# Other places for the softmax pieces of head pairs 6 to 8 in the first feed-forward batch of a fused attention and feed-forward kernel

## The chip, the core and the metric

One NeuronCore of a Trainium2 chip runs the whole program. The metric is the device time of one execution in microseconds (us); a kernel is told by the median of its runs. In the profile PE is TensorE (matmuls; PEld its weight loads), DVE is VectorE, ACT is ScalarE, POOL is GpSimd and SP is SyncE, which here issues most of the DMAs. L127 is line 127 of the kernel.

## The reference, cut to what matters

The attention has 8 batches, 8 heads, 512 local and 32 global positions and a head dimension of 64. A local position attends to the local positions within 32 of it and to the 32 global ones, a global position to all 544. The result goes through a feed-forward network with a softplus between its two products, all in float32.

```python
s_ll = scale * np.matmul(q_l, k_l.transpose(0, 1, 3, 2))
s_ll = np.where(mask, s_ll, -1000000000.0)        # |pos - pos'| <= 32
s_l = np.concatenate([s_lg, s_ll], axis=-1)
out_l = np.matmul(sm(s_l), np.concatenate([v_g, v_l], axis=2))
...
x = np.ascontiguousarray(attn_out.transpose(0, 2, 1, 3)).reshape(B * S, H * D)
h = x @ w_in                                       # 4352 x 512 by 512 x 2048
g = np.maximum(h, 0.0) + np.log1p(np.exp(-np.abs(h)))
return g @ w_out                                   # 4352 x 2048 by 2048 x 512
```

## The kernel before, in words

**Pairs and batches.** The 64 (batch, head) attentions are done two at a time: 32 head pairs, four to a batch of the feed-forward network. Pairs 0 to 5 are computed first, in a loop of their own. Pairs 6 to 31 are each cut into five *pieces*, which are written between the parts of the feed-forward work. Feed-forward batch 0 uses pairs 0 to 3, batch 1 pairs 4 to 7, batch 2 pairs 8 to 11; so pairs 6 and 7 have to be finished while batch 0 runs, and pair 8 while batch 1 runs.

**The pieces of a pair m** (list built in `pieces`, lines 425 to 446):
- `scores(m, 0)` and `scores(m, 1)` (L296): TensorE computes half of the scores each into `s_ps`, two banks of PSUM. For pairs 6 and 7 the mask is added by a matmul and ScalarE copies the half to the tile `s` (L322); for pair 8 VectorE adds the mask as it copies (L327). VectorE then takes maxima of blocks (L333). With each half go the loads of pair m+1's queries and keys (L288).
- `maxima(m)` and `probs(m, 0)`, `probs(m, 1)` (L364, L371): GpSimd moves the block maxima together (L354), VectorE folds them (L357 to L367) and spreads them into two tiles `mb` (L375); GpSimd subtracts them from `s` in seven instructions (L379), ScalarE exponentiates each half (L381), VectorE sums blocks (L385).
- `totals(m)` (L388): the same fold for sums, the reciprocals (L354, L357 to L361, L390, L391, L394) and `rb` (L396).
- `values(m)` and `normalise(m)` (L398, L411): TensorE multiplies by the values into `v_ps`; VectorE reads `v_ps` in L416, L417 and L418 and finishes in L419 and L421.

From the moment the feed-forward output banks exist, `s_ps` (of pairs up to 8) and `v_ps` take turns in one and the same pair of PSUM banks (pool `ps_a`, one buffer). So scores that are written behind a `values` can start only when L418 has read the values out.

**Feed-forward.** For each of 16 feature blocks f of a batch, TensorE computes `h_f` in two halves of six matmuls (`hpart`, L532), into two PSUM buffers taken in turn. ScalarE computes Abs, Exp and Ln into a tile `e` (L550 to L552), VectorE finishes softplus in L553, which is also the last reader of `h_f`: the matmuls of `h_f+2` wait for it. ScalarE rounds `e` to `gh` (L556), GpSimd computes the rest `gl` (L558), and the output products `o` of that block (`opart`, L561), twelve matmuls, read `gh` and `gl`; below, o(f) is that group of twelve. In batch 0 the writing order is h_0, h_1, h_2, o(0), h_3, o(1) and so on: one h, one o.

**Weights.** During the attention of pairs 0 to 5 and through batch 0, the weights are cut into a high and a low part, one tile of 128x512 after the other: a load by SP (L475), a ScalarE copy (L489), three VectorE instructions (L496, L498, L501, each on a 128x512 tile, called `wbits` and `raw`), a ScalarE rounding (L506) and two GpSimd subtractions (L508). Sixteen tiles are written before batch 0; the others are written in between the parts of batch 0, by lines 641 to 652 and 713.

**What sets the order.** Each piece has a number, its place; `SLOTS` (line 38) gives the five numbers of pairs 6, 7 and 8 in the order first scores, second scores, maxima with probabilities, totals, values. In batch 0 a running value `at` goes from 76 to 103.5 as the feed-forward parts are written, in batch 1 from 103.5 to 151.5, and a piece is written once `at` has reached its number:

```python
        at = first + 48 * (b + gone[b] / total[b]) if b else START + (first + 48 - START) * gone[b] / total[b]
        while pcs and pcs[0][0] <= at:
            pcs.pop(0)[1]()
```

Places under 76 (72 and 75 of pair 6) are taken in the loop before. The matmuls keep the order in which they are written (L126), and so do the loads of queries, keys and weights among themselves. Everything else is arranged by the framework's scheduler, which decides the row of each engine's instructions from the program, from the buffers and from its own estimates of time. The resulting row of each engine is fixed at build time; an instruction that waits holds up what stands behind it in its engine's row.

Of the kernel before, what the change touches and what calls it, by code (L numbers as in the profile page):

```python
# [34 lines left out]
TOT = 14  # L35
WIDE = 9
FIRST = 55.5
SLOTS = {6: (72, 75, 78, 86, 90), 7: (81, 87, 87, 97.5, 101.5), 8: (92, 98, 98, 109, 113.5)}
ORDER = "H O H H O G O H O H H O H O G O H O H H O H O G O H O H H O H H O G O O".split()
GW = 75  # L40
W_AHEAD = 13
# [18 lines left out]
def moe_over_global_local_attention(  # L60
# [235 lines left out]
    def scores(m, g):  # L296
        if "o" not in banks:
            ps = ps_s.tile([P, 2, 512], F32, tag=("oA", "oB")[g], name=f"s_ps{m}_{g}")
        elif m >= WIDE and g:
            ps = [ps_h.tile([P, 512], F32, tag="h", name=f"s_ps{m}_{g}_{h}") for h in range(2)]  # L300
        else:
            ps = ps_a.tile([P, 2, 512], F32, tag="a", name=f"s_ps{m}_{g}")
        half = (lambda h: ps[h]) if isinstance(ps, list) else (lambda h: ps[:, h])
        pe_mask = m < MPE
        cut = slice(512 * g, 512 * g + 512)
        for h in range(2 if pe_mask else 0):
            mm(half(h), lhsT=ident, rhs=mask[:, cut], start=True, stop=False, skip_group_check=True)
        for c, o, qs, w in CHUNKS:
            if not cut.start <= o < cut.stop:
                continue  # L310
            raw, ks, o = st["raw", m, c // 2], QW[c // 2] + 128 * (c % 2), o - cut.start
            for h in range(2):
                r = slice(64 * h, 64 * h + 64)
                mm(half(h)[:, o:o + w], lhsT=raw[r, ks:ks + P], rhs=raw[r, qs:qs + w],
                   start=not pe_mask, stop=True, skip_group_check=True)
        if g == 0:
            st["mt", m] = pl.tile([P, 348], F32, tag="mt", name=f"mt{m}", bufs=2)
            nc.gpsimd.memset(windows(st["mt", m], 0, 36, 3, 4), LOW)  # L318
            st["s", m] = pl.tile([P, 2, 1024], F32, tag="s", name=f"s{m}", bufs=2)
        s = st["s", m][:, :, cut]  # L320
        if pe_mask:
            nc.scalar.copy(s, ps)  # L322
        elif isinstance(ps, list):
            for h in range(2):
                nc.vector.tensor_tensor(s[:, h], ps[h], mask[:, cut], op=ALU.add)
        else:
            nc.vector.tensor_tensor(s, ps, mask[:, cut].unsqueeze(1).to_broadcast([P, 2, 512]), op=ALU.add)  # L327
        if m < WIDE:
            block_maxima(m, g)
# [95 lines left out]
    def pieces():  # L425
# [6 lines left out]
        for m in range(M0, M):  # L432
            g0, g1, mx, tot, val = SLOTS.get(m, (None, None, 12 * m + 5, 12 * m + TOT, 12 * m + VAL))
            for g, slot in ((0, g0), (1, g1)) if m in SLOTS else ():
                fs = [lambda m=m, g=g: scores(m, g)]
# [344 lines left out]
```

## Time and profile before

| What | Value |
|---|---|
| median of 3 runs | 977.25 us (977.24 to 977.72) |
| profiled execution, its own time | 979.5 us |
| span of the trace in it | 977.7 us |
| mean granted TensorE clock | 0.985 |
| TensorE busy | 948.4 us, 97% of the span |
| VectorE, ScalarE, GpSimd busy | 630.0, 502.4 and 451.1 us |
| first matmul of h_0 | 87.85 us from the span's start |

Times of the trace count from the span's start. A row of the timeline has the start, the duration, the engine, the line, the operation, the tiles (without their numbers), how many records it merges, and in brackets how long the engine had stood idle before and which instruction released it. The row of the waits has the total, the number of times and the longest.

### The profile page before, as it was taken

The numbers are of one execution on the slowest core, as the hardware profiler recorded it, in microseconds if no ns is written. First come the engines' busy times: TensorE is split into PE (matmuls) and PEld (weight loads), VectorE is DVE, ScalarE is ACT, GpSimd is POOL, SyncE is SP. The second block draws the span as 40 slices with busy tenths as digits, with TensorE's granted clock in tenths as the row PEclk, the third lists the DMA queues.
The fourth block names the chain that finished last, engine by engine and source line by source line (L and its number), as shares of the span: only waits on it lengthen the run. The fifth ranks groups of instructions, "written<-read, shape, count | busy, mean of one in ns | idle before, by whom it ended". The sixth has DMA issues, their size and how long they took to land.

```text
span 977.7 us, 14397 instructions
## 1 busy us (share of the span) xinstructions
PE 948.4 (97%) x5239; PEld 765.0 (78%) x5239; DVE 630.0 (64%) x1295; ACT 502.4 (51%) x890; POOL 451.1 (46%) x634
## 2 busy tenths in 40 slices
PE   6798999999999999999999999999999999999998
PEld 4676777778888888888888888888888888888896
DVE  6888959767677766786677667776677666211211
ACT  5786656644454444454454444544444446444553
POOL 5866858734444444353344444444425444222221
PEclk8898899999999999999999999999999999999999
DMA  9824222121112111121112111221112100100000
GB/s 357 321 78 163 87 76 72 60 76 50 38 30 93 50 50 50 50 93 49 35 47 96 29 38 50 79 64 50 50 50 80 45 18 18 50 1 1 15 30 22
DMA packets 34327, 66.21 MB, mean 68 GB/s; under 512 B 7632, under 2 KB 11472, under 8 KB 34256
## 3 DMA queue, kind: packets, MB, share of 16 engines
q1 hardware_dynamic: 33440, 65.19, 20.1%
q8 instruction: 41, 0.67, 0.3%
q14 instruction: 30, 0.25, 0.1%
q10 hardware_dynamic: 816, 0.10, 0.1%
HBM read 55.84 MB, written 9.44 MB: 67 GB/s over the span
## 4 chain that ended last, share of the span: by engine, by line
PE 85%; DVE 8%; ACT 2%; issue 2%; POOL 1%; DMA 1%; SPq 0%; POOLq 0%; ACTq 0%; DVEq 0%
PE o L127 37%; PE h L127 36%; PE s_ps L127 6%; PE v_ps L127 5%; DVE wbitswo L498 1%; ACT e L174 1%; DVE sums L171 1%; PE s L127 1%; DMA woraw<-in_w_out 1%; DVE woraw L501 1%; DVE wbitswo L496 1%; PE t L127 1%; DVE wbitswi L498 0%; DVE e L553 0%; PE s0g L127 0%
## 5 line engine op out<-in xcount | busy, mean ns | idle before, releaser
L127 PE MATMUL h<-xh,wi 128*128 128x512 f32 (+1 forms) x1152 | 346.6, 385 | 7.1 <-DVE e L553 7.1
L127 PE MATMUL o<-wo,gh 128*128 128x512 f32 x1088 | 345.5, 398 | 0.5 <-POOL wo L508 0.5
L558 POOL TENSOR_TENSOR gl<-e,gh 128x512 fp32r<-128x512 f32 (+1 forms) x152 | 181.8, 1200 | 265.9 <-ACT gh L556 234.8
L127 PEld LDWEIGHTS h<-xh,wi 128*128 128x128 f32 x1152 | 213.8, 190 | 53.0 <-DVE e L553 7.9
L127 PEld LDWEIGHTS o<-wo,gh 128*128 128x128 f32 x1088 | 200.1, 188 | 48.6 <-POOL wo L508 0.9
L127 PE MATMUL h<-xl,wi 128*128 128x512 f32 (+1 forms) x576 | 219.9, 382 | 0.2 <-DVE xl L462 0.2
L127 PE MATMUL o<-wo,gl 128*128 128x512 f32 x544 | 214.8, 395 | 0.2 <-POOL gl L558 0.2
L553 DVE SCALAR_TENSOR_TENSOR e<-h,e 128x512 f32<-128x512 f32 x136 | 92.7, 682 | 183.4 <-ACT e L552 165.5
L550 ACT ACTIVATE e<-h 128x512 f32<-128x512 f32 x136 | 80.9, 595 | 224.3 <-PE h L127 224.3
L379 POOL TENSOR_TENSOR s<-s,mb 128x320 f32<-128x320 f32 (+6 forms) x136 | 139.7, 1062 | 73.0 <-DVE mb L375 73.0
L556 ACT CAST gh<-e 128x512 fp32r<-128x512 f32 x136 | 83.9, 617 | 118.4 <-DVE e L553 118.2
L127 PEld LDWEIGHTS h<-xl,wi 128*128 128x128 f32 x576 | 109.1, 189 | 23.3 <-DVE xl L462 0.7
L127 PEld LDWEIGHTS o<-wo,gl 128*128 128x128 f32 x544 | 102.2, 188 | 24.7 <-POOL gl L558 1.2
L552 ACT ACTIVATE e<-e,one 128x512 f32<-128x512 f32 x136 | 98.4, 723 | 4.0
L385 DVE TRANSPOSE_TENSOR_REDUCE zt<-s 128x32 f32<-128x1024 f32 x52 | 64.7, 1243 | 49.0 <-ACT s L381 49.0
L551 ACT ACTIVATE e<-e 128x512 f32<-128x512 f32 x136 | 85.9, 631 | 2.9
L381 ACT ACTIVATE s<-s 128x1024 f32<-128x1024 f32 x52 | 55.1, 1059 | 30.5 <-POOL mt L318 24.8
L333 DVE TRANSPOSE_TENSOR_REDUCE mt<-s 128x32 f32<-128x1024 f32 x52 | 64.7, 1245 | 6.2 <-ACT s L322 4.6
L127 PEld LDWEIGHTS s_ps<-raw 64*128 64x128 f32 x728 | 54.6, 187 | 11.4 <-issue 8.9
L354 POOL COPY mt<-mt 32x75 f32<-32x75 f32 x78 | 19.3, 247 | 93.8 <-DVE mt L333 91.6
L127 PE MATMUL s_ps<-raw 64*128 64x192 f32 (+3 forms) x728 | 60.2, 308 | 0.2
L375 DVE STREAM_TRANSPOSE mb<-mt 128x512 f32<-128x512 f32 (+1 forms) x104 | 52.6, 563 | 0.7
(131 smaller groups left out, 872.6 us busy)
## 6 DMA issues: line engine op xcount, KB each, us to landing
raw<-in_qk SPq DMA_DIRECT2D x52, 272.0 KB, 3.1
v<-in_v SPq DMA_DIRECT2D x26, 384.0 KB, 3.0
out<-ot SPq DMA_DIRECT2D x34, 256.0 KB, 2.2
wiraw<-in_w_in SPq DMA_DIRECT2D x16, 512.0 KB, 9.3
woraw<-in_w_out SPq DMA_DIRECT2D x16, 512.0 KB, 8.4
raw<-in_qk SPq DMA_DIRECT2D x26, 224.0 KB, 3.4
v<-in_v SPq DMA_DIRECT2D x6, 512.0 KB, 7.5
raw<-in_qk SPq DMA_DIRECT2D x6, 416.0 KB, 8.6
```

Of the source, the lines that this page charges most:

```text
L127: order["pe"] = after(nc.tensor.matmul(*a, **k), "pe").ins
L333: order["scores"] = nc.vector.tensor_reduce(windows(st["mt", m], 4 + 16 * g, 36, 2, 16), s.rearrange("p h (b k) -> p h b k", k=32), axis=A ...
L375: nc.vector.transpose(mb[:, :, o:o + 32 * n].rearrange("p h (s k) -> p h s k", k=32), windows(e, k, 21, 2, n).unsqueeze(3).to_broadcast([P ...
L379: nc.gpsimd.tensor_tensor(s[:, h, o:o + w], s[:, h, o:o + w], mb[:, h, q:q + w], op=ALU.subtract)
L381: nc.scalar.activation(s, s, AF.Exp, scale=0.125)
L385: nc.vector.tensor_reduce(windows(st["zt", m], 4 + 16 * g, 36, 2, 16), s.rearrange("p h (b k) -> p h b k", k=32), axis=AX.X, op=ALU.add, a ...
L550: nc.scalar.activation(e, ph, AF.Abs)
L551: nc.scalar.activation(e, e, AF.Exp, scale=-1.0)
L552: nc.scalar.activation(e, e, AF.Ln, bias=one)
L553: nc.vector.scalar_tensor_tensor(e, ph, 0.0, e, op0=ALU.max, op1=ALU.add)
L556: nc.scalar.copy(gh, e)
L558: nc.gpsimd.tensor_tensor(gl[:, c], e[:, c], gh[:, c].bitcast(F32), op=ALU.subtract)
```

## The change

Line 38 alone is changed. The numbers are the places of the pieces of pairs 6, 7 and 8:

```diff
-SLOTS = {6: (72, 75, 78, 86, 90), 7: (81, 87, 87, 97.5, 101.5), 8: (92, 98, 98, 109, 113.5)}
+SLOTS = {6: (72, 75, 80.5, 88, 92), 7: (82, 85, 85.5, 95, 99), 8: (92.5, 97, 97, 108, 112.5)}
```

Pair 6's maxima, totals and values come later by 2 to 2.5. Pair 7's first scores come 1 later, its other four pieces 1.5 to 2.5 sooner. Pair 8's first scores come 0.5 later, the others 1 sooner. No instruction is added or taken away; the scheduler arranges VectorE's, ScalarE's, GpSimd's and SP's rows anew. The numbers behind the names of tiles differ, since the tiles are counted in another order.

**Place 1: VectorE at the start of batch 0, up to e_0.** `mt_945` and `mb` are the maxima of pair 6; `wbits`, `wiraw` and `woraw` are weight tiles; `e_0` is the softplus of h_0. Before:

```order
L367 COPY mt_945<-mt_945 32x42 x3
L496 TENSOR_SCALAR wbitswi_1235<-wbitswi_1235 128x512
L375 STREAM_TRANSPOSE mb_0_1137<-mt_945 128x2x256
L375 STREAM_TRANSPOSE mb_0_1137<-mt_945 128x2x160
L375 STREAM_TRANSPOSE mb_1_1147<-mt_945 128x2x192 x2
L498 SCALAR_TENSOR_TENSOR wbitswi_1235<-wiraw_1065,wbitswi_1235 128x512
L496 TENSOR_SCALAR wbitswo_1327<-wbitswo_1327 128x512
L501 SCALAR_TENSOR_TENSOR wiraw_1065<-wiraw_1065,wbitswi_1235 128x512
L496 TENSOR_SCALAR wbitswo_1354<-wbitswo_1354 128x512
L498 SCALAR_TENSOR_TENSOR wbitswo_1327<-woraw_1069,wbitswo_1327 128x512
L553 SCALAR_TENSOR_TENSOR e_0_1086<-h_0_1073,e_0_1086 128x512
```

And now, the last twelve rows up to the same instruction:

```order
L361 COPY mt_945<-mt_945 32x6
L501 SCALAR_TENSOR_TENSOR wiraw_1065<-wiraw_1065,wbitswi_1205 128x512
L498 SCALAR_TENSOR_TENSOR wbitswo_1178<-woraw_1063,wbitswo_1178 128x512
L367 COPY mt_945<-mt_945 32x42 x3
L496 TENSOR_SCALAR wbitswo_1327<-wbitswo_1327 128x512
L501 SCALAR_TENSOR_TENSOR woraw_1063<-woraw_1063,wbitswo_1178 128x512
L496 TENSOR_SCALAR wbitswo_1354<-wbitswo_1354 128x512
L375 STREAM_TRANSPOSE mb_0_1231<-mt_945 128x2x256
L375 STREAM_TRANSPOSE mb_0_1231<-mt_945 128x2x160
L498 SCALAR_TENSOR_TENSOR wbitswo_1327<-woraw_1069,wbitswo_1327 128x512
L375 STREAM_TRANSPOSE mb_1_1241<-mt_945 128x2x192 x2
L553 SCALAR_TENSOR_TENSOR e_0_1086<-h_0_1073,e_0_1086 128x512
```

Pair 6's maxima were spread (L375) soon after their fold, and three rows of one weight tile and three of two others stood around them. Now rows of five weight tiles are mixed into the fold and the spreading. Counted from the first L357 of the fold (it stands a few rows higher) to `e_0`, there are six L496, L498 and L501 before and nine now; three more now stand right ahead of that L357 (L496 and L498 of the tile `woraw_169`, L496 of `wiraw_1065`).

On GpSimd, ahead of `gl_0` (L558), there stood before the two L508 of one weight tile between the seven L379 of pair 6 and `gl_0`. Now two weight tiles' L508 stand ahead of the first L379, two L508 of a third (`wo_1183`) behind the first L379, then the other six L379, and then `gl_0`.

**Place 2: TensorE where pair 6's values are computed.** `v_ps` are those values, `s_ps_0` the first scores of pair 8. Before, the values are followed by h_9:

```order
L127 MATMUL v_ps_1586<-s_947,v_147 64x160 x2
L127 MATMUL v_ps_1586<-s_947,v_147 64x192 x8
L127 MATMUL v_ps_1586<-s_947,v_147 64x96 x2
L127 MATMUL h_9_1609<-xh_0_367,wi_1025 128x512 x2
L127 MATMUL h_9_1609<-xl_0_368,wi_1025 128x512
L127 MATMUL h_9_1609<-xh_1_474,wi_1025 128x512 x2
L127 MATMUL h_9_1609<-xl_1_475,wi_1025 128x512
L127 MATMUL h_9_1609<-xh_2_585,wi_1044 128x512 x2
```

The first scores of pair 8 followed only after the rest of h_9, o(7) and the first half of h_10. Now the values stand in the middle of h_10, and the scores right behind it:

```order
L127 MATMUL v_ps_1648<-s_947,v_147 64x160 x2
L127 MATMUL v_ps_1648<-s_947,v_147 64x192 x8
L127 MATMUL v_ps_1648<-s_947,v_147 64x96 x2
L127 MATMUL h_10_1641<-xh_2_585,wi_1286 128x512 x2
L127 MATMUL h_10_1641<-xl_2_586,wi_1286 128x512
L127 MATMUL h_10_1641<-xh_3_750,wi_1286 128x512 x2
L127 MATMUL h_10_1641<-xl_3_751,wi_1286 128x512
L127 MATMUL s_ps_0_1696<-raw_0_1304 128x160 x2
L127 MATMUL s_ps_0_1696<-raw_0_1304 128x192 x2
L127 MATMUL s_ps_0_1696<-raw_1_1395 128x160 x2
```

The values moved behind h_9, o(7) and half of h_10; between them and pair 8's scores, which use the same banks, six matmuls are left.

**Place 3: VectorE where it reads these values out.** `xa_2` and `lap` are results of pair 6, `zt_1444` (before: `zt_1489`) are pair 7's sums. Before:

```order
L553 SCALAR_TENSOR_TENSOR e_8_1553<-h_8_1540,e_8_1553 128x512
L385 TENSOR_REDUCE zt_1489<-s_1267 128x2x16
L416 TENSOR_TENSOR xa_2_1599<-v_ps_1586,rb_1428 128x256
L417 TENSOR_TENSOR lap_1600<-v_ps_1586,rb_1428 128x64
L496 TENSOR_SCALAR wbitswo_1565<-wbitswo_1565 128x512
L418 TENSOR_TENSOR xa_2_1599<-v_ps_1586,rb_1428 128x352
L419 TENSOR_TENSOR xa_2_1599<-xa_2_1599,lap_1600 128x64
L498 SCALAR_TENSOR_TENSOR wbitswo_1565<-woraw_1352,wbitswo_1565 128x512
L421 TENSOR_REDUCE lap_1600<-xa_2_1599 128x32
L385 TENSOR_REDUCE zt_1489<-s_1267 128x2x16
```

And now:

```order
L498 SCALAR_TENSOR_TENSOR wbitswo_1620<-woraw_1475,wbitswo_1620 128x512
L390 TENSOR_SCALAR zt_1444<-zt_1444 32x42
L501 SCALAR_TENSOR_TENSOR woraw_1475<-woraw_1475,wbitswo_1620 128x512
L391 RECIPROCAL zt_1444<-zt_1444 32x42
L553 SCALAR_TENSOR_TENSOR e_9_1610<-h_9_1586,e_9_1610 128x512
L394 COPY zt_1444<-zt_1444 32x21
L496 TENSOR_SCALAR wbitswo_1687<-wbitswo_1687 128x512
L394 COPY zt_1444<-zt_1444 32x21 x2
L498 SCALAR_TENSOR_TENSOR wbitswo_1687<-woraw_1502,wbitswo_1687 128x512
L416 TENSOR_TENSOR xa_2_1661<-v_ps_1648,rb_1538 128x256
L417 TENSOR_TENSOR lap_1662<-v_ps_1648,rb_1538 128x64
L418 TENSOR_TENSOR xa_2_1661<-v_ps_1648,rb_1538 128x352
```

L416 to L418 of pair 6 stood behind e_8; now they stand behind e_9 and behind nearly all of the totals of pair 7. Counted from the first L357 of pair 7's maxima, there stand ahead of the end of L418 now six L496, six L498, five L501, both L385 of pair 7, e_7 to e_9, the fold of the totals with L390, L391 and L394. Before, the stretch from that L357 up to and with e_10 held five L496, five L498, five L501, both L385, e_8 to e_10, the same fold with L390, L391 and L394, pair 6's L416 to L421, and also L396, L327 and one L333. That L357 itself stood behind e_7 and now stands behind e_6.

## The prediction

> **What bounds the kernel now.** I read the page first, then TensorE's waits, its timeline around the longest of them, the granted clock there, and the rows of VectorE and GpSimd ahead of them.
>
> ```profile
> PE 948.4 (97%) x5239; PEld 765.0 (78%) x5239; DVE 630.0 (64%) x1295; ACT 502.4 (51%) x890; POOL 451.1 (46%) x634
> PE h L127 <- DVE e L553: 7.1, 2, 4.8
> PE h L127 <- DVE xl L462: 0.2, 1, 0.2
> PE o L127 <- POOL wo L508: 0.5, 1, 0.5
> PE o L127 <- POOL gl L558: 0.2, 1, 0.2
> ```
>
> TensorE is the bound, and the change leaves its work alone; so the time can change only by TensorE's waits and clock. From h_0 on it waits twice for L553 and for 0.9 us more at the end of batch 0. The two waits, and the clock behind each (third last figure of a stretch: granted clock):
>
> ```profile
> 99.89 1.22 PE L127 MATMUL h<-xh,wi 128*128 128x512 f32 x2 [4.78 <-DVE e L553]
> 104.99 0.63 PE L127 MATMUL o<-wo,gh 128*128 128x512 f32 x2
> 107.75 0.62 PE L127 MATMUL h<-xh,wi 128*128 128x512 f32 x2
> 167.15 0.73 PE L127 MATMUL h<-xh,wi 128*128 128x512 f32 x2 [2.31 <-DVE e L553]
> 100.00:104.00 4.00, 4.00 (x10) 3.13 (x11) 4.00 (x5) 2.64 (x4) 3.42 (x4) 0.50 0.01 2
> 168.00:172.00 4.00, 4.00 (x19) 3.14 (x18) 3.40 (x4) 3.80 (x7) 4.00 (x6) 1.00 0.00 2
> ```
>
> Wait one (4.78 us, for e_0, ahead of h_2) costs more than itself: h_2 takes 5.10 us at half clock, where the twelve matmuls behind it take 2.76. Wait two (2.31, for e_10, ahead of h_12) leaves the clock full. Neither h is late; VectorE's queue is:
>
> ```profile
> 97.76 1.48 DVE L498 SCALAR_TENSOR_TENSOR wbitswo<-woraw,wbitswo 128x512 int32<-128x512 int32 x1
> 161.88 0.72 ACT L552 ACTIVATE e<-e,one 128x512 f32<-128x512 f32 x1
> 166.41 0.68 DVE L553 SCALAR_TENSOR_TENSOR e<-h,e 128x512 f32<-128x512 f32 x1
> ```
>
> The second L553 starts 3.8 us after the end of the Ln it needs, the first behind weight rows as slow as 1.48. What counts is which VectorE rows stand ahead of a row that TensorE waits for.
>
> **Part one: the start.** Pair 6's fold starts at 88.97 after 1.63 us of idle time.
>
> ```profile
> 85.93 0.69 DVE L498 SCALAR_TENSOR_TENSOR wbitswi<-wiraw,wbitswi 128x512 int32<-128x512 int32 x1
> 88.97 0.54 DVE L357 TENSOR_REDUCE mt<-mt 32x12 f32<-32x96 f32 x2 [1.63 <-POOL mt L354]
> L498 DVE SCALAR_TENSOR_TENSOR wbitswo<-woraw,wbitswo 128x512 int32<-128x512 int32 x8 | 7.8, 978 | 0.0
> L501 DVE SCALAR_TENSOR_TENSOR woraw<-woraw,wbitswo 128x512 int32<-128x512 int32 x8 | 6.6, 829 | 0.0
> L496 DVE TENSOR_SCALAR wbitswo<-wbitswo 128x512 int32<-128x512 int32 x8 | 6.5, 806 | 0.0
> L496 DVE TENSOR_SCALAR wbitswi<-wbitswi 128x512 int32<-128x512 int32 x7 | 3.3, 471 | 1.1 <-ACT wbitswi L489 0.9
> ```
>
> Means are over 85 to 170 us; a row starts about 0.07 before its forerunner's record ends, so I take L496 0.58, L498 0.91, L501 0.77. The three added ahead of the fold take 2.1, the idle time hides 1.6, 0.4 is left. Behind the fold one L498 and two L501 more: 2.45. That makes e_0 2.9 later at most. The other end: before, L379 ran beside this stretch from 92.55 on and L498 took 1.48; now L379 waits for a spreading that stands further back. With every weight row of the stretch near 0.69 and 0.43 I come to 0.9 sooner. I take the middle, **+0.9**.
>
> Behind it, o(0) needs `gl_0`:
>
> ```profile
> 142.32 2.02 DVE L375 STREAM_TRANSPOSE mb<-mt 128x512 f32<-128x512 f32 x4
> 101.54 1.88 POOL L558 TENSOR_TENSOR gl<-e,gh 128x256 fp32r<-128x256 f32 x2
> L508 POOL TENSOR_TENSOR wi<-wiraw,wi 128x256 fp32r<-128x256 f32 x5 | 4.1, 828 | 0.5 <-POOL mt L354 0.5
> 92.55 7.14 POOL L379 TENSOR_TENSOR s<-s,mb 128x320 f32<-128x320 f32 x7 [1.65 <-DVE mb L375]
> L379 POOL TENSOR_TENSOR s<-s,mb 128x320 f32<-128x320 f32 x1 | 0.9, 886 | 1.6 <-DVE mb L375 1.6
> ```
>
> Now L379 (0.9), two L508 (1.7), the other six L379 (7.14 less 0.89: 6.3) and half of L558 (0.9) follow the first spreading, which ends 3.0 ahead of e_0 (three L375 of 0.5, an L498 of 0.9 and e_0's own 0.6 lie between): `gl_0` comes 6.8 after e_0. TensorE asks for it 5.6 after e_0 (h_2 at half clock 5.1, two matmuls 0.5). A new wait of 1.2, or none with the shorter rows; I take **+0.7**. Before, `gl_0` was there at 103.42 and asked for 0.5 behind 104.99.
>
> **Part two: pair 8's first scores.** They use the banks that L418 empties. TensorE's reach first:
>
> ```profile
> 136.42 0.62 PE L127 MATMUL o<-wo,gh 128*128 128x512 f32 x2
> 138.79 0.69 DVE L553 SCALAR_TENSOR_TENSOR e<-h,e 128x512 f32<-128x512 f32 x1 [1.46 <-ACT e L552]
> 139.40 0.54 DVE L357 TENSOR_REDUCE mt<-mt 32x12 f32<-32x96 f32 x2
> 144.84 1.96 PE L127 MATMUL v_ps<-s,v 128*64 128x160 f32 x24
> 146.72 0.73 PE L127 MATMUL h<-xh,wi 128*128 128x512 f32 x2
> 149.72 0.50 DVE L418 TENSOR_TENSOR xa<-v_ps,rb 128x352 f32<-128x352 f32 x1
> 152.40 0.63 PE L127 MATMUL h<-xh,wi 128*128 128x512 f32 x2
> 153.88 1.14 PE L127 MATMUL s_ps<-raw 64*128 64x160 f32 x12
> ```
>
> From the end of h_6 to these scores there are now o(4), h_7, o(5), h_8, o(6), h_9, o(7) at 2.8 (136.42 to 144.84 holds o(5), h_8 and o(6)), h_10 in halves of 1.5 (152.40 to 153.88) and the values, 1.9: 24.5 us. VectorE: h_7 ended at 136.42, its L553 started 2.4 later, the next row 0.6 behind that; so pair 7's fold, now behind e_6, starts 3.0 after the end of h_6. From the fold to the end of e_10 VectorE never paused: 139.40 to 167.09, 27.7 us. The new stretch up to L418 is that one, plus one L496 and L498 (0.58 + 0.91), less these five:
>
> ```profile
> L333 DVE TRANSPOSE_TENSOR_REDUCE mt<-s 128x32 f32<-128x1024 f32 x4 | 5.0, 1242 | 4.6 <-ACT s L322 4.6
> L396 DVE STREAM_TRANSPOSE rb<-zt 128x640 f32<-128x640 f32 x2 | 1.6, 818 | 0.0
> L327 DVE TENSOR_TENSOR s<-s_ps,mask 128x1024 f32<-128x1024 f32 x1 | 1.2, 1205 | 0.0
> L419 DVE TENSOR_TENSOR xa<-xa,lap 128x64 f32<-128x64 f32 x1 | 0.3, 339 | 0.0
> L421 DVE TENSOR_REDUCE lap<-xa 128x32 f32<-128x96 f32 x1 | 0.3, 251 | 0.0
> ```
>
> 1.17 + 0.75 + 1.16 + 0.27 + 0.18 = 3.5; 27.7 + 1.5 - 3.5 = 25.7. L418 ends 28.7 after h_6, TensorE stands there from 24.5 on: **+4.2**. Before, L418 ended at 150.22, 3.7 ahead of need. Bounds: all 17 weight rows near the short rows take 4 off and there is no wait; all at 1.15 put 5.8 on. GpSimd has as many rows beside it as before, so I hold to the measured stretch.
>
> [...]
>
> **Wait two goes: -2.3.** L501, L419, L421, L396, L496, L498, L327, L501 and e_10 follow L418, 6.1 us by the rows above; TensorE has the scores (1.1), o(8), h_11 and o(9) to do, 9.5. It is 3.4 early.
>
> **The clock behind the new wait.** The 4.78 was followed by half clock, the 2.31 was not. Early in the kernel, where TensorE is often idle, the same eight matmuls took 1.94 behind 3.04 us of waiting and 1.06 behind 0.22:
>
> ```profile
> 18.05 1.94 PE L127 MATMUL t<-identf,e 128*128 128x128 f32 x8 [3.04 <-issue]
> 27.32 1.06 PE L127 MATMUL t<-identf,e 128*128 128x128 f32 x8 [0.22 <-issue]
> ```
>
> 4.2 is nearest to 4.78, so I add its loss, 5.10 - 2.76: **+2.3**; 0 at the other end.
>
> **The end of batch 0.** Of the 0.9 us of small waits, one is for the last weight tile's L508, now written further ahead: **-0.5** (0.9 less to 0.5 more).
>
> At nothing: the loads behind pair 8's first one leave later by the h_4 that pair 7's scores were moved behind, 2.8, and by the 1.6 of the start; a weight load among them may make e_5 that much late. h_7 asks for its buffer only three units (8.4 us) behind h_5, of which softplus needs 2.4 and 0.7: 5.3 are left to cover 4.4. Without that cover the excess would be paid. Pair 8's values stand one h sooner in batch 1, where VectorE has no weights left to cut.
>
> **Sum:** 0.9 + 0.7 + 4.2 + 2.3 - 2.3 - 0.5 = +5.3 on the profiled execution's 979.5 us (span 977.7 and 1.8 around it). The median, 977.25, lies 2.25 below that execution; I put the same difference on it: **982.5 us**.
>
> **Rivals.**
> - *The clock stays full* behind the new wait, as behind 2.31: +3.0, 980.2 us. The point lies somewhere between 2.3 and 4.8 us of wait. [...] Chance 0.27.
> - *The new wait only replaces wait two.* If VectorE's stretch takes 23.5 in place of 25.7, TensorE waits 2.0 with its clock kept: 1.6 + 2.0 - 2.3 - 0.5 = +0.8, 978.0 us. For it: rows of 0.69 exist; against: 27.7 measured without a gap. Chance 0.16.
> - *VectorE keeps up and the kernel is faster.* With the stretch at 21.5 or less there is no wait at the scores; wait two and the small ones go, and e_0 comes at the early end without a wait for `gl_0`: between 1.6 - 2.8 = -1.2 and -0.9 - 2.8 = -3.7, middle -2.5, 974.8 us. It needs the short row length for nearly all weight rows while GpSimd is busy. Chance 0.12.
>
> **How the numbers follow.** The forecast with its size keeps 0.45. A measurement tells about 0.2%, 2 us, from no change. Slower by more: forecast and first rival, 0.72; within: 0.16; faster: 0.12. The range goes from 976.5, which leaves out most of the last rival, to 986.5 (all bounds a little on the long side); some 0.2 lie outside.
>
> **What would show it.** In the new profile: a wait of s_ps for L418 (or L417) of 2 to 6 us near 160 us; no wait of an h near 167; wait one within a few us of 4.8 with half clock behind it; a wait for `gl_0` under 2 us. I am wrong if TensorE reaches pair 8's scores without a wait, or if VectorE from pair 7's fold to L418 takes under 22 us; and on the start if e_0's L553 starts before 98 or after 103.

## The result and the profile after

The kernel after takes 983.34 us (median; 982.13 to 985.08) beside 977.39 for the one before (977.24 to 977.72): ratio 1.0063, 95% interval 1.0051 to 1.0074. It is slower by 0.6%, and the interval leaves out no change; the forecast was 982.5. The profiled execution is the longest of the four, one of 985.08 us with a span of 983.1 and a granted clock of 0.983.

TensorE's waits in the kernel after (us in total, times, longest), the lines that differ from before:

```profile
PE h L127 <- DVE e L553: 6.5, 2, 5.9
PE s_ps L127 <- issue: 4.6, 1, 4.6
...
PE o L127 <- POOL gl L558: 1.5, 1, 1.5
```

Wait two and the small waits at the end of batch 0 are no longer in the list; a wait of `s_ps` and one for `gl` are new. TensorE's timeline says where (start, length, then in brackets the idle time ahead and what ended it):

```profile
100.24 1.22 PE L127 MATMUL h<-xh,wi 128*128 128x512 f32 x2 [5.86 <-DVE e L553]
...
106.83 0.51 PE L127 MATMUL o<-wo,gl 128*128 128x512 f32 x1 [1.48 <-POOL gl L558]
...
109.26 0.63 PE L127 MATMUL h<-xh,wi 128*128 128x512 f32 x2
...
152.59 0.72 PE L127 MATMUL h<-xh,wi 128*128 128x512 f32 x2 [0.66 <-DVE e L553]
...
162.35 2.08 PE L127 MATMUL s_ps<-raw 64*128 64x160 f32 x12 [4.62 <-issue]
```

From the top: wait one ahead of h_2 (4.78 before), the new wait of o(0) for `gl_0`, the start of h_3, a small wait of h_10 for e_8, and the 4.62 us at pair 8's first scores. The view names nobody for the last one ("issue"), but VectorE's timeline shows what ended just before. Its rows for pair 6's fold, e_0, pair 7's fold and the last read of pair 6's values:

```profile
88.86 0.54 DVE L357 TENSOR_REDUCE mt<-mt 32x12 f32<-32x96 f32 x2
...
99.54 0.65 DVE L553 SCALAR_TENSOR_TENSOR e<-h,e 128x512 f32<-128x512 f32 x1
...
135.30 0.54 DVE L357 TENSOR_REDUCE mt<-mt 32x12 f32<-32x96 f32 x2
...
161.74 0.51 DVE L418 TENSOR_TENSOR xa<-v_ps,rb 128x352 f32<-128x352 f32 x1
```

L418 ends at 162.25, the scores start at 162.35. In every run below that waits there, the scores start 0.1 us after L418's end. From pair 7's fold to the end of L418 VectorE takes 26.95 us.

The granted clock around that wait, cut where it changes (length of the stretch; busy us of PE, PEld, DVE, ACT, POOL with their counts; granted clock third from the end):

```profile
154.97:158.38 3.41, 2.76 (x24) 1.91 (x18) 3.35 (x7) 2.80 (x5) 3.41 (x4) 1.00 0.00 0
158.38:161.79 3.41, 0.00 (x0) 0.00 (x0) 3.33 (x7) 0.60 (x1) 3.41 (x5) 1.00 0.18 22
161.79:165.21 3.42, 2.86 (x14) 2.47 (x15) 3.38 (x8) 1.24 (x3) 2.29 (x4) 0.50 0.71 256
165.21:168.62 3.41, 3.41 (x9) 2.64 (x9) 3.41 (x5) 2.16 (x5) 2.05 (x3) 0.50 0.28 82
168.62:172.03 3.41, 3.41 (x16) 2.79 (x16) 3.34 (x4) 0.81 (x2) 3.27 (x4) 1.00 0.00 0
```

The wait ends at 162.35; two stretches of 3.41 us at half clock end only at 168.62.

**One ledger for all runs.** Each profiled execution is cut at three moments: the second L333 of pair 6 on VectorE (84.10 before, 83.35 after), the start of h_2 (99.89, 100.24) and the start of h_3 (107.75, 109.26); then comes the rest of the span. What lies ahead of the first moment is the same work in all kernels and takes 80.89 to 84.10 us in the fourteen traces, so it is left out. In the last column is the difference of the medians to the kernel before on the same chip.

| Kernel | L333 to h_2 | h_2 to h_3 | h_3 to the end | median |
|---|---|---|---|---|
| before | 15.79 | 7.86 | 869.95 | |
| after | 16.89 | 9.02 | 873.84 | +5.95 |
| after, run again | 16.97 | 10.23 | 873.07 | +7.57 |
| pair 6 old (p6old) | 15.61 | 7.19 | 867.95 | -2.41 |
| only pair 6 new (p6new) | 17.40 | 9.00 | 872.33 | +5.21 |
| values at 90 (val90) | 17.42 | 9.01 | 867.90 | +1.12 |
| maxima at 78 (mx78) | 15.64 | 7.31 | 873.10 | +2.99 |
| scores later (s8late95) | 16.89 | 9.01 | 868.03 | +1.88 |
| two tiles less (drop2) | 17.42 | 8.99 | 870.10 | +3.17 |
| p6old, 16 matmuls added | 15.61 | 7.19 | 868.43 | -2.44 |
| p6old, 22 matmuls added | 15.64 | 7.22 | 867.88 | -2.48 |
| mx78, 18 matmuls added | 15.63 | 7.24 | 871.04 | +1.08 |
| only pair 7 new (p7only) | 15.63 | 7.19 | 870.30 | -0.14 |
| only pair 8 new (p8only) | 15.78 | 7.48 | 868.35 | -0.99 |

### The profile page after: what moved, and what is told of

It is laid out like the page before. It is cut to its first block, busy times and chain, and to the rows that moved or that the text cites. A ratio compares the mean times of both kernels' runs of the same rounds, so it can differ in the third digit from the quotient of the medians.

```text
span 983.1 us, 14407 instructions
## 1 busy us (share of the span) xinstructions
PE 948.7 (97%) x5239; PEld 766.6 (78%) x5239; DVE 630.6 (64%) x1295; ACT 501.7 (51%) x890; POOL 452.4 (46%) x634
## 4 chain that ended last, share of the span: by engine, by line
PE 87%; DVE 6%; ACT 3%; POOL 2%; issue 2%; POOLq 0%; ACTq 0%; DVEq 0%
PE o L127 39%; PE h L127 37%; PE s_ps L127 6%; PE v_ps L127 5%; ACT e L174 1%; POOL s L379 1%; DVE sums L171 1%; DVE wbitswo L498 1%; DVE wiraw L501 1%; DVE wbitswi L498 1%; DVE woraw L501 0%; DVE wbitswo L496 0%; PE s0g L127 0%; PE s L127 0%; POOL wo L508 0%
## 5 line engine op out<-in xcount | busy, mean ns | idle before, releaser
L558 POOL TENSOR_TENSOR gl<-e,gh 128x512 fp32r<-128x512 f32 (+1 forms) x152 | 180.7, 1193 | 279.3 <-ACT gh L556 246.2
L379 POOL TENSOR_TENSOR s<-s,mb 128x320 f32<-128x320 f32 (+6 forms) x136 | 138.4, 1053 | 70.0 <-DVE mb L375 70.0
L127 PEld LDWEIGHTS o<-wo,gl 128*128 128x128 f32 x544 | 102.6, 189 | 25.7 <-POOL gl L558 1.9
L385 DVE TRANSPOSE_TENSOR_REDUCE zt<-s 128x32 f32<-128x1024 f32 x52 | 64.7, 1244 | 51.7 <-ACT s L381 51.6
L333 DVE TRANSPOSE_TENSOR_REDUCE mt<-s 128x32 f32<-128x1024 f32 x52 | 64.7, 1244 | 5.8 <-ACT s L322 4.1
L375 DVE STREAM_TRANSPOSE mb<-mt 128x512 f32<-128x512 f32 (+1 forms) x104 | 52.7, 562 | 0.7
```

Source lines behind the costliest of these rows:

```text
L127: order["pe"] = after(nc.tensor.matmul(*a, **k), "pe").ins
L333: order["scores"] = nc.vector.tensor_reduce(windows(st["mt", m], 4 + 16 * g, 36, 2, 16), s.rearrange("p h (b k) -> p h b k", k=32), axis=A ...
L375: nc.vector.transpose(mb[:, :, o:o + 32 * n].rearrange("p h (s k) -> p h s k", k=32), windows(e, k, 21, 2, n).unsqueeze(3).to_broadcast([P ...
L379: nc.gpsimd.tensor_tensor(s[:, h, o:o + w], s[:, h, o:o + w], mb[:, h, q:q + w], op=ALU.subtract)
L385: nc.vector.tensor_reduce(windows(st["zt", m], 4 + 16 * g, 36, 2, 16), s.rearrange("p h (b k) -> p h b k", k=32), axis=AX.X, op=ALU.add, a ...
L558: nc.gpsimd.tensor_tensor(gl[:, c], e[:, c], gh[:, c].bitcast(F32), op=ALU.subtract)
```

## The experiments

Each kernel is the one after with the edit that is shown; `SLOTS` is its line 38. The theory is the prediction's: VectorE's row up to L418 sets when the banks of pair 8's first scores come free, pair 6's later maxima set the start, and half clock follows the wait. Each text that was on record before the run is quoted.

**Pair 6 as before, the rest new.**

```diff
-SLOTS = {6: (72, 75, 80.5, 88, 92), 7: (82, 85, 85.5, 95, 99), 8: (92.5, 97, 97, 108, 112.5)}
+SLOTS = {6: (72, 75, 78, 86, 90), 7: (82, 85, 85.5, 95, 99), 8: (92.5, 97, 97, 108, 112.5)}
```

> Pair 6's three places as before (78, 86, 90), those of pairs 7 and 8 as in the change. Theory (VectorE's row up to L418 sets when the banks of pair 8's first scores are free; the start's terms come from pair 6's later maxima): L418 stands 7.7 us sooner behind pair 7's fold than in the change (17.6 against 25.3 by the row lengths), so the wait of 4.62 for s_ps is gone; e_10 comes about in time, so wait two (2.31) is gone or under 1; wait one is back at 4.8 and the wait for gl_0 is gone; the 0.9 of small waits at the batch's end stay gone. 977.4 - 2.3 - 0.9 = 974.2, up to 975.2 with some of wait two left: faster than before. Rival A (the sooner places of pairs 7 and 8 are what costs): 980 to 983, with a wait of 3 us or more near 160 us. Rival B (nothing but the start costs): 977.4, as before.

Measured: 975.44 beside 977.85, ratio 0.9977 (0.9968 to 0.9986), a little above what was expected. TensorE's rows for h_2, pair 8's first scores and h_12:

```profile
98.16 1.22 PE L127 MATMUL h<-xh,wi 128*128 128x512 f32 x2 [4.58 <-DVE e L553]
...
152.90 1.14 PE L127 MATMUL s_ps<-raw 64*128 64x160 f32 x12
...
163.53 0.74 PE L127 MATMUL h<-xh,wi 128*128 128x512 f32 x2 [1.02 <-DVE e L553]
```

The scores start without a wait, wait two is 1.02 in place of 2.31, and no wait for `gl_0` is left. This table is faster than both kernels. The sooner places of pairs 7 and 8 bring 2.0 us (h_3 to the end: 867.95 beside 869.95); rivals A and B are both out.

**Pair 6 new, the rest as before.**

```diff
+SLOTS = {6: (72, 75, 80.5, 88, 92), 7: (81, 87, 87, 97.5, 101.5), 8: (92, 98, 98, 109, 113.5)}
```

> Pair 6's three places as in the change (80.5, 88, 92), those of pairs 7 and 8 as before. Theory: pair 6's later values alone bring the wait at pair 8's first scores, which now stand right behind the values: L418 is 17.6 behind pair 7's fold, which itself is one h later (behind e_7), so some 27 after the end of h_6, where TensorE asks at 24: a wait of 3 to 4 us for s_ps, with 0 to 2.3 of half clock behind it; the start's terms as in the change (+2.0); wait two gone (-2.3); end waits as before. 977.4 + 2.0 + 3.5 + (0 to 2.3) - 2.3 = 980.6 to 982.9. Rival A (pairs 7 and 8's sooner places cost, pair 6's do not, beyond the start): 977 to 979.5, without a wait over 1.5 us at the scores. Rival B (the start is the whole cost): 983 with no wait at the scores.

Measured: 983.06 beside 977.85, 1.0057 (1.0045 to 1.0070): nearly the whole loss of the change, just above the 980.6 to 982.9 that was expected. `gl_0`, the values and the scores behind them:

```profile
105.35 0.49 PE L127 MATMUL o<-wo,gl 128*128 128x512 f32 x1 [0.81 <-POOL gl L558]
...
151.79 1.96 PE L127 MATMUL v_ps<-s,v 128*64 128x160 f32 x24
...
158.36 2.08 PE L127 MATMUL s_ps<-raw 64*128 64x160 f32 x12 [4.61 <-issue]
```

The values end at 153.75 and the scores stand right behind them. L418 (157.76, 0.50 long) ends 0.1 ahead of the scores here too.

**One number each: the values at 90 (val90, the first line), the maxima at 78 (mx78, the second).**

```diff
+SLOTS = {6: (72, 75, 80.5, 88, 90), 7: (82, 85, 85.5, 95, 99), 8: (92.5, 97, 97, 108, 112.5)}
```

```diff
+SLOTS = {6: (72, 75, 78, 88, 92), 7: (82, 85, 85.5, 95, 99), 8: (92.5, 97, 97, 108, 112.5)}
```

> The change with one number back: pair 6's values at 90 in place of 92. Theory: L418 stands 17.6 instead of 25.3 behind the fold, the wait of 4.62 at pair 8's first scores and the half clock behind it (1.3 to 2.3) go, the 0.66 of h_10 too; 0 to 1 us of wait two may come back. The start stays as slow as in the change (wait one 5.9, gl_0 1.5). 983.3 - 4.6 - 0.7 - 1.8 + 0.5 = 976.7, between 975.5 and 978. Rival (the start is the larger cost, and the wait at the scores only swallows time that is lost otherwise): 981 to 983.

> The change with another number back: pair 6's maxima at 78 in place of 80.5. Theory: wait one falls from 5.86 to 4.8, the wait for gl_0 (1.48) goes, h_0 starts 0.5 later as before; the wait at pair 8's first scores stays at 4 to 5 us. 983.3 - 1.1 - 1.5 + 0.5 = 981.2, between 980 and 982.5. Rival (the start is the larger cost): 978 or less.

Measured, beside the same 977.85: val90 978.97, 1.0012 (1.0003 to 1.0020); mx78 980.84, 1.0029 (1.0018 to 1.0040). In val90, `gl_0` and the scores:

```profile
106.58 0.50 PE L127 MATMUL o<-wo,gl 128*128 128x512 f32 x1 [0.43 <-POOL gl L558]
...
156.44 1.14 PE L127 MATMUL s_ps<-raw 64*128 64x160 f32 x12
```

In mx78, h_2 and the scores:

```profile
98.39 1.22 PE L127 MATMUL h<-xh,wi 128*128 128x512 f32 x2 [6.10 <-DVE e L553]
...
158.81 2.08 PE L127 MATMUL s_ps<-raw 64*128 64x160 f32 x12 [4.63 <-issue]
```

The two numbers take the change apart. With the values at 90, everything behind h_3 is as in p6old (867.90 beside 867.95) and the start is slow; with the maxima at 78 the start is as in p6old and the wait at the scores stays. The values' place costs 5.2 us (mx78 less p6old behind h_3) to 5.9 (after less val90). The maxima's place costs 1.8 up to h_2 and 1.8 more from h_2 to h_3 (val90 less p6old), which is more than the 2.1 that mx78's text takes off for it. val90 came out above its range for another reason: its text takes 6.6 off the median of the change (983.34), but its sizes were read from the traced execution of the change, the longest one (985.08); from there to the traced execution of val90 (978.92) it is 6.2.

**The scores later, L418 as late as in the change.**

```diff
+SLOTS = {6: (72, 75, 80.5, 88, 92), 7: (82, 85, 85.5, 95, 99), 8: (95.2, 97, 97, 108, 112.5)}
```

> The change with pair 8's first scores two and a half units later (95.2 in place of 92.5: behind o(8), h_11 and o(9), 8.4 us of TensorE's work); pair 6's values stay at 92 and VectorE's row up to L418 stays as long. Theory (what costs is that the banks are asked for before L418 empties them): L418 is as late as in the change, but nobody waits for it; the 4.62 at the scores and the half clock behind it (1.2 to 2 us) go, 0 to 1 us for e_10 ahead of h_12 may come; the start as slow as in the change. 983.3 - 4.6 - 1.5 + 0.5 = 977.7, between 976.5 and 979. Rival (VectorE's row itself is what the kernel waits for, by way of the softplus behind it, whatever place the scores have): the wait turns up at h_12 with 3 us or more, 981 to 983.

Measured: 979.39 beside 977.51, 1.0018 (1.0009 to 1.0026). VectorE's L418, and behind it TensorE's rows for the scores, h_12 and the second scores:

```profile
161.99 0.51 DVE L418 TENSOR_TENSOR xa<-v_ps,rb 128x352 f32<-128x352 f32 x1
```

```profile
166.07 1.14 PE L127 MATMUL s_ps<-raw 64*128 64x160 f32 x12
168.01 0.73 PE L127 MATMUL h<-xh,wi 128*128 128x512 f32 x2 [0.80 <-DVE e L553]
...
174.77 1.34 PE L127 MATMUL s_ps<-raw 64*128 64x32 f32 x16 [0.93 <-DVE s L327]
```

L418 is as late as in the change (26.5 us behind pair 7's fold at 135.49, up to its start; 26.4 in the change), and nobody waits for it. So a late L418 costs nothing by itself; the shared banks, asked for too early, are the cost. Behind h_3 the run is where p6old is (868.03). The total is 0.4 above its range, again because 5.6 was taken off the median of the change and not off its traced execution: from the 985.08 of that one to the 979.27 of this run's it is 5.8.

**Less work on VectorE ahead of L418.**

```diff
         lo32, hi32 = t[:, :, 0], t[:, :, 1]
+        if (kind, k) in (("wo", 11), ("wi", 13)): return hi32.bitcast(F32)
```

> The change, with VectorE's six rows for two weight tiles (wo 11 and wi 13) left out, so that these tiles hold other numbers; all six stood between pair 7's fold and L418, and the order of the rest moves a little. Theory (the wait is as long as VectorE's row): by the row lengths L418 comes 3.8 us sooner behind the fold; the wait of 4.62 falls to about 0.8 and keeps the clock, the 0.66 of h_10 goes; the start stays. 983.3 - 3.8 - 0.7 - 1.5 = 977.3, between 976 and 979.5. Rival (L418 waits for something else: the spread reciprocals, the values): the wait stays over 3 us, 981 to 983.

Measured: 980.68 beside 977.51, 1.0029 (1.0018 to 1.0039), above the range. VectorE's second L385 of pair 7 and L418, then the scores:

```profile
146.47 1.25 DVE L385 TRANSPOSE_TENSOR_REDUCE zt<-s 128x32 f32<-128x1024 f32 x1 [2.38 <-ACT s L381]
...
158.88 0.52 DVE L418 TENSOR_TENSOR xa<-v_ps,rb 128x352 f32<-128x352 f32 x1
```

```profile
159.50 1.72 PE L127 MATMUL s_ps<-raw 64*128 64x160 f32 x12 [2.51 <-issue]
```

L418 starts 24.0 us behind the fold (134.86) in place of 26.4, and the wait fell by 2.1, from 4.62 to 2.51; TensorE itself came 0.3 sooner, since its wait of h_10 fell from 0.66 to 0.36. The wait did not fall by 3.8, because VectorE, with less to do, now stands 2.38 us idle for an Exp of ScalarE ahead of that L385. The 2.51 us were still followed by half clock from 159.92 to 163.33.

**The clock behind the new wait.** In mx78, 18 matmuls are added ahead of the scores; `hpart` then takes h_11's tile from `st`:

```diff
+    warm = lambda t: [mm(t, lhsT=ident, rhs=mask[:, 0:512], start=True, stop=True, skip_group_check=True) for _ in range(18)]
...
-        pe_mask = m < MPE
+        pe_mask = m < MPE; (m, g) == (8, 0) and warm(st.setdefault("h11", ps_h.tile([P, 512], F32, tag="h", name="h0_11")))
```

> The table with pair 6's maxima back at 78 (run before: 980.84, wait of 4.63 at pair 8's first scores, no wait for gl_0), and 18 matmuls of 512 columns ahead of those scores, into the bank of h_11, which h_11 overwrites: some 4 us inside the wait. VectorE's order up to L418 is the same; behind it e_10 stands ahead of L327. Theory on the clock: the scores and the o behind them run at full clock, 1.2 to 2 us less: 979.2, between 978.5 and 979.8; the start of the scores stays where it was. Rival (the clock behind the wait costs nothing, since VectorE is late anyway): 980.8.

Measured: 978.59 beside 977.51, 1.0009 (1.0000 to 1.0018), where mx78 had 1.0029. The added matmuls and the scores:

```profile
152.16 4.06 PE L127 MATMUL h<-mask,ident 128*128 128x512 bf16 x17
156.97 1.14 PE L127 MATMUL s_ps<-raw 64*128 64x160 f32 x12 [0.76 <-issue]
```

The scores take 1.14 in place of 2.08 and the clock stays full. Behind h_3 the run is 2.1 us shorter than mx78 (871.04 beside 873.10). VectorE's row behind L418 is not quite the same in the two runs (e_10 stands ahead of L327 here), but in neither trace does TensorE wait for anything between these scores and 260 us. The loss of clock behind this wait is real and about 2 us.

**The clock behind wait one.** In p6old, 16 and then 22 matmuls are added ahead of h_2, into the bank of o_0 (`warm` as above, with 16 and 22):

```diff
-            ph = g["ps", b, f]
+            ph = g["ps", b, f]; (b, f, js) == (0, 2, (0, 1)) and warm(output_banks().tile([P, 512], F32, tag="o0", name="warm"))
```

> The first run's table (pair 6's places as before, 7 and 8 as in the change), and 16 matmuls of 512 columns ahead of h_2, into the bank of o_0, which o_0 overwrites: some 3.5 us of TensorE's work inside wait one, of which the kernel uses nothing. Theory on the clock (half clock follows from TensorE's idle time): wait one is left with about 1 us, h_2 runs at full clock; from h_2 to h_3 5.6 us in place of 7.2, so 975.4 - 1.6 = 973.8, between 973 and 974.5. Rival (the clock falls with time or load, not with idling): 975.4, with h_2 still at half clock; or 977 if the added matmuls are in the way.

> As the run with 16 added matmuls ahead of h_2, but with 22 (some 4.8 us in place of 3.4). Theory (the clock falls when most of one 3.41 us stretch of the grid is idle; 2.58 idle were enough, 1.32 were not): the rest of the wait is 0 to 1.3 us, h_2 runs at full clock, h_2 to h_3 5.6 us in place of 7.2: 975.4 - 1.6 = 973.8; up to 0.6 more where h_1 ends late and the added matmuls outlast the wait. Rival (the clock follows something other than TensorE's idling): 975.4 with half clock in h_2, as with 16.

Measured: 975.07 beside 977.51, 0.9970 (0.9958 to 0.9982), and 975.66 beside 978.14, 0.9971 (0.9960 to 0.9981). Neither differs from p6old's 0.9977 by more than the intervals, and both are above the 973.8 that was expected. With 16 the added work left 2.58 us of waiting, and the clock fell all the same. TensorE's rows, and the stretches before and after the fall:

```profile
91.90 3.40 PE L127 MATMUL warm<-mask,ident 128*128 128x512 bf16 x15
97.88 0.73 PE L127 MATMUL h<-xh,wi 128*128 128x512 f32 x2 [2.58 <-DVE e L553]
```

```profile
95.20:98.61 3.41, 0.83 (x4) 0.64 (x4) 3.41 (x4) 1.94 (x5) 3.41 (x6) 1.00 0.01 2
98.61:102.03 3.42, 3.42 (x10) 2.66 (x9) 3.42 (x5) 2.01 (x3) 2.80 (x3) 0.50 0.00 0
```

With 22 the clock stayed full, and h_2 took 2.86 us. TensorE's rows for the added matmuls, h_2, o(0) and h_3, and VectorE's e_1:

```profile
93.98 4.70 PE L127 MATMUL warm<-mask,ident 128*128 128x512 bf16 x21
98.50 0.73 PE L127 MATMUL h<-xh,wi 128*128 128x512 f32 x2
...
101.36 0.62 PE L127 MATMUL o<-wo,gh 128*128 128x512 f32 x2
...
105.72 0.73 PE L127 MATMUL h<-xh,wi 128*128 128x512 f32 x2 [1.46 <-DVE e L553]
```

```profile
104.99 0.68 DVE L553 SCALAR_TENSOR_TENSOR e<-h,e 128x512 f32<-128x512 f32 x1
```

Here the theory on the clock holds, and the price put on it does not: h_3 starts 7.22 us after h_2 with full clock and 7.19 with half clock, because e_1 is ready no sooner (in p6old h_3 starts at 105.35, and e_1 ended at 105.29). What the clock gave, a new wait of 1.46 took.

**Pair 7 alone (p7only, the first line), pair 8 alone (p8only, the second).**

```diff
+SLOTS = {6: (72, 75, 78, 86, 90), 7: (82, 85, 85.5, 95, 99), 8: (92, 98, 98, 109, 113.5)}
```

```diff
+SLOTS = {6: (72, 75, 78, 86, 90), 7: (81, 87, 87, 97.5, 101.5), 8: (92.5, 97, 97, 108, 112.5)}
```

> Only pair 7's places as in the change (82, 85, 85.5, 95, 99), 6 and 8 as before. Theory (VectorE's row ahead of e_10 sets wait two): e_10 is 31.7 behind pair 7's fold by the row lengths, 2.1 later than with pair 8 moved as well (29.6, where 1.02 was waited); wait two about 3.1, with 0 to 1.7 of half clock: 975.4 + 2.1 + (0 to 1.7) = 977.5 to 979.2. Rival (pair 7's sooner places alone bring the gain): 975 to 976.

> Only pair 8's places as in the change (92.5, 97, 97, 108, 112.5), 6 and 7 as before. Theory: pair 7's fold stands behind e_7 as before, e_10 comes 26.1 behind it in place of 27.3: wait two 1.1 in place of 2.3, some of the 0.9 at the batch's end gone: 977.5 - 1.2 - 0.5 = 975.8. Rival (pair 7's places carry the gain): 977 to 978.

Measured, beside 978.14: p7only 978.00, 0.9995 (0.9986 to 1.0004); p8only 977.15, 0.9996 (0.9986 to 1.0005). Wait two in p7only, and the stretches of the clock around it:

```profile
163.57 0.73 PE L127 MATMUL h<-xh,wi 128*128 128x512 f32 x2 [2.42 <-DVE e L553]
```

```profile
161.28:164.69 3.41, 1.12 (x5) 0.94 (x6) 2.83 (x4) 2.42 (x5) 1.53 (x3) 1.00 0.00 0
164.69:168.10 3.41, 3.41 (x10) 2.63 (x9) 2.65 (x3) 2.49 (x5) 3.02 (x4) 0.50 0.00 0
```

In p8only it is 1.55:

```profile
164.54 0.73 PE L127 MATMUL h<-xh,wi 128*128 128x512 f32 x2 [1.55 <-DVE e L553]
```

Neither pair alone shows a gain beyond its interval; both together brought 0.23%. For pair 8 that is not the last word: its median is 0.99 us lower, the ratio says 0.04%, and behind h_3 its trace is 1.6 us shorter than that of before (868.35 beside 869.95), most of the 2.0 of both together. How much of the gain pair 8's places bring alone stays open. p7only came as expected (wait two 2.42 where 3.1 was estimated, with half clock behind it), p8only less than expected: 1.55 of wait two was left where I had 1.1.

**The change once more.** The kernel after without an edit.

> The change itself, once more, beside the others of this call. Theory (the granted clock changes only on a grid of 3.41 us that runs free of the program, so the same wait is followed by one or two stretches of half clock): the times fall into two groups about 2.5 us apart, near 982 and 984.6, and the profiled run has half-clock stretches of 3.4, 6.8 or 10.2 us and no others. Rival (the spread is of VectorE's or GpSimd's row lengths): a continuous spread, and e_0 or L418 late by the same amount where the run is long.

Measured: 985.71 beside 978.14, 1.0070 (1.0056 to 1.0084). The times are 983.92, 984.00, 985.71, 985.96 and 986.16: two groups about 2 us apart, each above where I had put it. Behind wait one and behind the scores the clock is half for 3.41 and 6.83 us. TensorE's rows:

```profile
100.70 1.22 PE L127 MATMUL h<-xh,wi 128*128 128x512 f32 x2 [4.35 <-DVE e L553]
...
108.53 0.50 PE L127 MATMUL o<-wo,gl 128*128 128x512 f32 x1 [2.89 <-POOL gl L558]
...
164.04 2.08 PE L127 MATMUL s_ps<-raw 64*128 64x160 f32 x12 [4.62 <-issue]
```

The wait at the scores is the same to the hundredth; the start is not: `gl_0` came 1.2 us later behind h_2 than in the other trace of this kernel. Each of the two times that this kernel ran, only one execution has a trace, so which group had which stretches of half clock is not shown.

## Why the prediction was right, point by point

- **The start, e_0 +0.9:** from L333 to h_2 the change takes 1.10 longer than before (16.89 less 15.79), and 1.6 in p6new, val90 and drop2; with the maxima at 78 it is 0.0 to 0.2 shorter. The cause, the place of pair 6's maxima, is right. The size says little: +0.9 was the middle of bounds from 0.9 sooner to 2.9 later, and which rows are slow in this stretch was not worked out.
- **`gl_0` +0.7:** the wait is 1.48, and h_2 to h_3 takes 1.16 longer than before. Right in cause, too small: the slow end of the bound (1.2) was the better value, and against p6old, which has one half-clock stretch here where before has two, the difference is 1.8. All six traces with the maxima at 80.5 have this wait (0.43 to 2.89), no trace with the maxima at 78 has it.
- **The new wait +4.2:** 4.62 (4.61 to 4.63 in the four traces that have it with VectorE's full work). The row from fold to L418 was put at 25.7 and took 26.95; TensorE itself came 0.66 later by a wait of h_10 for e_8 that was not in the working, so the two errors partly cancel. The shared banks are shown as the cause by s8late95, VectorE's row as the length by val90 and drop2.
- **Its clock +2.3:** about 2 us by the added matmuls (2.0 by the ratios, 2.1 by the ledger), measured in mx78 and not in the change itself. The rival that the clock stays full is out for this wait. The choice between the two was in part luck: it went by the length of the wait (4.2 is nearest to 4.78), and length alone does not decide, as the next but one section shows. My estimate from the stretches there: a wait of 4.6 leaves at least 2.3 us of itself in one stretch of 3.41, however the edges cut it, and 2.29 was enough to lose the clock; the 4.2 of the forecast could have left 2.1, for which no trace here has a case.
- **Wait two -2.3:** gone in the change, since TensorE itself is late there. In p6old, where TensorE is not late, 1.02 of it is left.
- **The end of batch 0, -0.5:** all of the 0.9 is gone.
- **The sum:** +5.3 was forecast, +5.95 measured. By the ledger it is 1.10 + 1.16 + 3.89 = +6.15 for the trace. The last term stands for 4.2 + 2.3 - 2.3 - 0.5 = 3.7 of the prediction; the rest of the difference is the start (2.26 for 1.6).
- **The rivals:** a wait that only replaces wait two, and VectorE keeping up, would have shown 2 us or no wait at the scores. Both are out.

Two remarks of the prediction do not stand. "Wait one costs more than itself" was read from h_2's 5.10 us at half clock; the run with 22 added matmuls shows that at this place e_1 holds h_3 back anyway, so that of the loss only what reaches past e_1 counts (7.86 in the trace of before, with two half-clock stretches, against 7.19 with one). That entered no term of the sum, as both kernels have wait one. And there is no length of wait between 2.3 and 4.8 us from which on the clock is lost: 2.42 (p7only) and 2.51 (drop2) lost it, and 2.89 (the change run again, for `gl_0`) kept it.

Two figures of the working do not come out when they are redone, and neither of them changes the sum. L327 less 0.07 is 1.13 and not 1.16; 17 rows at 1.15 put 5.6 on and not 5.8. The stretch itself took 1.25 more than was forecast.

## What to carry to other kernels

When a piece is moved, list what shares its buffer and compare two moments: when the last reader empties it, and when the next writer's engine gets there; a late reader costs only if the writer is asked for sooner, and moving the writer back by a few units of work is worth as much as moving the reader forward (behind h_3 s8late95 takes 868.03 us and val90 867.90). Split a change that moves several pieces: here one pair's old places with the two others' new ones beat both tables, though neither of the two shows a gain beyond its interval alone. A stall or a stretch of half clock ahead of work that another engine holds back anyway is not worth removing: with 22 matmuls added to p6old h_2 kept its clock, and h_3 came 7.22 us behind it in place of 7.19.

## What the runs showed of the hardware

**The clock moves on a grid.** In all fourteen traces, every half-clock stretch between 86 and 180 us that begins and ends there is 3.41, 6.83 or 10.24 us long, one to three times 3.41, and within a trace the edges lie whole multiples of 3.41 apart (in the change, the falls at 96.94 and 161.79: 64.85, 19 times 3.413). The grid did not keep step with the program: the fall just ahead of this part, at 82.77 to 85.34 us, lay between 0.35 us ahead of the start of pair 6's second L333 (the change run again) and 2.77 us behind it (val90). In this part of the traces the clock of a stretch followed TensorE's busy time in the one ahead. It fell after stretches in which TensorE was busy 0.00 to 1.12 of 3.41 us and did not fall after 1.78 or more; it rose after 3.02 or more, but for one stretch of which a third went into products of 64 columns, and stayed low after 2.86 or less. So the same idle time can lose the clock or not. Wait two before, 2.31 us, was cut by an edge into 1.32 and 0.99:

```profile
162.75:166.16 3.41, 2.09 (x10) 1.39 (x8) 3.37 (x6) 0.66 (x1) 0.46 (x2) 1.00 0.54 152
166.16:169.57 3.41, 2.42 (x11) 2.00 (x12) 3.34 (x5) 2.93 (x5) 2.26 (x3) 1.00 0.00 0
```

The 2.42 us of p7only lay with 2.29 in one stretch, and half clock followed. The 2.89 us for `gl_0` in the second run of the change were cut into 1.63 and 1.26, and the clock stayed full:

```profile
103.86:107.28 3.42, 1.78 (x8) 1.13 (x6) 2.81 (x4) 2.17 (x4) 3.42 (x6) 1.00 0.01 2
107.28:110.69 3.41, 2.16 (x9) 1.80 (x10) 3.34 (x5) 2.65 (x4) 3.41 (x6) 1.00 0.02 5
```

These limits hold for this part only. Just ahead of it, at 82.8 to 85.3 us, the clock fell in all fourteen traces after stretches in which the profile shows TensorE busy for 1.6 to 3.4 us; there it also computes products of 64 columns (`o0g`). So the busy time of the profile does not decide by itself, and what the clock goes by is not shown.

**Rows beside each other change in length.** In the change VectorE's weight rows ran at 0.67 us while two L508 of GpSimd beside them took 4.28; a few us later a weight row took 1.23 beside two L508 that took 1.63 together. Two rows of VectorE and then two of GpSimd, one of each case:

```profile
89.61 0.67 DVE L501 SCALAR_TENSOR_TENSOR woraw<-woraw,wbitswo 128x512 int32<-128x512 int32 x1
94.38 1.23 DVE L501 SCALAR_TENSOR_TENSOR woraw<-woraw,wbitswo 128x512 int32<-128x512 int32 x1
```

```profile
88.83 4.28 POOL L508 TENSOR_TENSOR wi<-wiraw,wi 128x256 fp32r<-128x256 f32 x2 [0.18 <-POOL mt L354]
93.42 1.63 POOL L508 TENSOR_TENSOR wo<-woraw,wo 128x256 fp32r<-128x256 f32 x2 [0.31 <-ACT wo L506]
```

Why it changes is not shown. A mean length per instruction was good to 5% over 27 us here (25.7 for 26.95), but it says nothing about which of the two engines has the long rows in a given stretch.

**The first 84 us vary.** The same work ahead of pair 6's second L333 took 80.89 to 84.10 us in the fourteen traces. The spread goes with the clock: with 3.4 us of half clock ahead of that moment it took 80.89 to 82.75, with 6.8 82.55 and 82.86, with 10.2 to 10.6 83.35 to 83.73, and with 13.7 (before) 84.10. A single profiled execution can therefore lie 2 us off its kernel's median for reasons that have nothing to do with the edit, and stages behind a common row are the safer comparison.
